# Linear attention and a gated feed-forward on one core: a k^T v product ahead of an attention run, weight sums beside chunk 0, and another order of a first layer's last steps

## The chip, the core and the metric

The kernel runs on one core of a Trainium2 chip. The engines of the core work side by side, each in its own order of instructions: TensorE (PE in the profile, its weight loads PEld), VectorE (DVE), ScalarE (ACT), GpSimd (POOL) and SyncE (SP, which here only issues DMAs). The metric is the time of the device in microseconds for one execution of the whole program; lower is better. Several runs are made and their median is told.

## The reference

```python
kv = np.einsum('bhsd,bhse->bhde', k, v)              # 8 batches, 8 heads, 576 tokens, 64 wide
out = np.einsum('bhsd,bhde->bhse', q, kv)
rms = np.sqrt(np.mean(out * out, axis=-1, keepdims=True) + 1e-06)
attn = (out / rms * g_norm)
x = np.ascontiguousarray(attn.transpose(0, 2, 1, 3)).reshape(4608, 512)
gate = 1.0 / (1.0 + np.exp(-(x @ w_gate)))           # 512 x 1536
val = x @ w_val                                      # 512 x 1536
return gate * val @ w_out                            # 1536 x 512
```

The weights come as 64-bit numbers and the rest as 32-bit ones; the kernel computes in 32 bits.

## The kernel before

**Chunks.** The 4608 tokens of the feed-forward are nine chunks of 512. The attention of batch b+1 is computed in pieces between the products of chunk b, since chunk b+1 needs its tokens. Chunk 0 uses plain products. Chunks 1 to 8 use a fast scheme with 26 products of block sums in place of 32 plain block products, for the first layer (gate and value, three column blocks j = 0, 1, 2) and for the second. Such a product needs *forms*: sums of blocks of the tokens (made by VectorE), of the hidden blocks h (`h_sums`, line 728: GpSimd, and for the last column block partly VectorE), of the first layer's weights (`w1_sums`, line 744, 28 sums of 128x256 for each column block, GpSimd, L747 in the profile) and of the second layer's weights (`w_form`, L1029 and L1031).

**The order is written by hand.** Every engine executes its instructions in the order in which the program text issues them. Around chunk 0 this order comes from the text `places` (line 802). Chunk 0's eleven tiles after the first have eight matmuls each; place p is the p-th of these 88 matmuls, 0.86 us apart, and behind it the named steps are issued: `CV` is one step of converting a weight unit (line 247), `KV2` the k^T v of batch 2, `D` the two ScalarE copies of it to `kvq` (L399, L400), `au ... ax1` and `bu ... bx1` the first and second attention run of batch 1 (products, squares, sums, root, norms, turns), `W0` the sums of first-layer weights of column block 0. In chunks 1 to 8 the steps are keyed to p, the number of the first layer's product (26 for each column block, 0 to 77), or to the place in the second layer.

**Converting weights.** A unit holds two 128x512 blocks. It takes five steps on VectorE (L197, L212, L224, L228, then L235 or L237) with two on ScalarE between them (L202 after the first, L217 after the second). Units 0 to 11 are the gate and value weights in the order of chunk 0's tiles: tile f needs unit f. Units 12 to 17 are the rows of the second layer's weights, two blocks each, in the order of chunk 0's second layer (L830 in the profile). `plain` (line 606) gives two PSUM banks to a tile; ScalarE's sigmoid (L599) and VectorE's product (L602) give them back.

**k^T v.** `kv_mm` (line 379, L388 and L395 in the profile) reads k and v from the tile h_more and writes a PSUM tile called `at`, which the attention runs use too, one after the other. The sums of first-layer weights write into parts of h_more, so they wait for the matmuls of batch 2's k^T v to read k and v. `kvq` holds the k^T v that the attention run's products (`u_mm`, L434) read.

**A first layer's end.** `PRODUCTS1` (line 671) lists 26 products: the PSUM region that a product adds to, the two forms, and the steps of `combine` (line 908) behind it. A step such as `o4=o4+K` adds region K to a piece of h (VectorE, L924), `s0` is a sigmoid (ScalarE, L913), and `o4*o0` multiplies value and gate (L916: GpSimd, but VectorE behind the very last product). Five PSUM banks go round: a region's bank is free once the last step that reads it is done. The second layer (L1058) starts at once; its first four regions take the bank of E, J, D and H of the first layer's end, in this order, and the product of its fourth region stands eighth and ninth among its first blocks of two matmuls each. The form 8 of h needs `o5`, form 9 needs `o7`, form 18 `o6` and `o4`.

**Chunk 1.** The weight sums of column block 2 are made late: 20 after the conversion's buffers are given up (line 885), and eight in chunk 1, one with each of p = 26 to 33 (lines 986, 987). There too the second layer's weight forms are made, on VectorE and GpSimd, each written over a piece of the first layer's weights that is used up and has been saved to DRAM, and each then stored to DRAM by SyncE.

Of the kernel before, what the change touches and what calls it, by code (L numbers as in the profile page):

```python
# [10 lines left out]
FP32 = mybir.dt.float32  # L11
# [9 lines left out]
def kernel(  # L21
# [11 lines left out]
    nc = tc.nc  # L33

    B, H, S, HD = q.shape
    T, DM = out.shape
    DF = moe_w_gate.shape[1]
    P = 128
# [17 lines left out]
    NRUN = NHP // 2  # L56
# [6 lines left out]
    NFT = DF // P  # L63
# [9 lines left out]
    const = ctx.enter_context(tc.tile_pool(name="const", bufs=1))  # L73
# [193 lines left out]


    kvq = const.tile([P, 2, NRUN, 2, HD], FP32, name="kvq")

    qTs = const.tile([P, QW], FP32, name="qTs")
    sqs = const.tile([P, 2 * NU * P], FP32, name="sqs")
# [102 lines left out]
    def feed(b):  # L375

        d = {}

        def kv_mm():
# [11 lines left out]
            for e in range(2):  # L391
                for m in range(NRUN):
                    for g in range(2):
                        rs, c = slice(PH * m, PH * m + PH), HD * (2 * g + e)
                        nc.tensor.matmul(ps[HD * g:HD * g + HD, m, e], rest[rs, c:c + HD],  # L395
                                         rest[rs, GH + c:GH + c + HD], start=False, stop=True, skip_group_check=True)

        def kv_copy():
            nc.scalar.copy(out=kvq[:, 0], in_=d["kv"])  # L399
            nc.scalar.copy(out=kvq[0:HD, 1], in_=d["kv"][HD:P])  # L400
# [82 lines left out]
            return ([u_mm, u_square, lambda: u_sum(0), lambda: u_sum(1), u_root] + norms +  # L483
                    [lambda i=i: x_turn(i) for i in range(NC)])

        kv = [kv_mm, kv_copy]
        t0, t1 = ([lambda m=m, e=e: turn(m, e) for e in range(2)] for m in range(NRUN))
        u0, u1 = heads_run(0), heads_run(1)
        if b == 1:
# [4 lines left out]
        where = """0:t00 5:t01 25:u0 26:q0 28:t10 30:s00,s01 33:t11 35:r0 36:n00 37:n01 39:n02 40:n03 42:n04 43:n05 44:n06  # L494
                   51:x00 52:x01 53:u1 56:q1 57:s10,s11 60:r1 62:n10,n11 63:n12 65:n13 66:n14 68:n15 69:n16""" if b == 2 else """
                   5:t00 8:t01 28:u0 29:t10 30:q0 33:s00,s01 36:r0 39:t11 41:n00 47:n01 51:x00,x01 54:u1
                   56:q1,s10,s11 61:r1 64:n10,n11""" if b == 3 else """
                   3:t00 7:t01 28:u0,t10 30:q0,s00,s01 37:r0 39:t11 47:n00,n01 53:x00,x01 54:u1
                   56:q1,s10,s11 60:r1 61:n10 63:n11"""
        first = [(int(w_.split(":")[0]), steps_[x]) for w_ in where.split() for x in w_.split(":")[1].split(",")]  # L500
# [133 lines left out]
    for token in order.split():  # L634
        name = token.rstrip("0123456789.")
        n = [int(i) for i in token[len(name):].split(".")]
        f = n[0]
# [10 lines left out]
        else:  # L648
            a[f][steps[name]]()
            if token == f"Q{NE - 1}":  # L650
# [10 lines left out]
    W_ORDER = (21, 24, 17, 18, 16, 25, 19, 42, 27, 34, 35, 36, 23, 29, 33, 20, 41, 28, 26, 40, 32, 38, 39, 43, 30, 37, 22,  # L661
               31)
# [17 lines left out]
    PRODUCTS2 = (("A", 8, 4, "o5=A"), ("C", 9, 1, "o4=C"), ("B", 18, 10, "o3=B"), ("A", 24, 14, "o1=A"),  # L680
# [7 lines left out]
    NPR = len(PRODUCTS2)  # L688
# [46 lines left out]
    NPA = len(PARTS)  # L735
    GW = 7 * 2 * P

    W1_FIRST = 20
    w1_more = [[] for _ in range(N3)]

    def w1_slot(j, s_):
# [2 lines left out]
    def w1_sums(j, some=slice(None)):  # L744
        for v in W_ORDER[some]:
            x, sign, y = SUMS[v]
            nc.gpsimd.tensor_tensor(out=w1_slot(j, w_at[v]), in0=w1_slot(j, w_at[x]), in1=w1_slot(j, w_at[y]),  # L747
                                    op=op_of(sign))
# [29 lines left out]
    def w1_form(c, j, part, v):  # L778
        if c == 1:
# [11 lines left out]
    spare_sg = sgs.pop()  # L791
    batch1, second_batch = feed(1), feed(2)
    named = {"LL": lambda: load_late(1), "LL2": lambda: load_late(2), "KV": batch1[0][0], "KV2": second_batch[0][0],
             "W0": lambda: w1_sums(0), "CV": convert_step}
    named.update({"C": batch1[0][1], "D": second_batch[0][1]})
    for i in range(NRUN):
        named[f"Q{i}"] = lambda i=i: load_q_run(1, i)
# [1 line left out]
    for i, which in enumerate("ab"):  # L799
# [3 lines left out]
        1:CV,CV 2:CV,Q0 4:CV,CV 5:CV,CV 6:CV,LL 7:CV,CV 10:CV,CV 11:Q1 15:CV 16:CV,CV 17:t00  # L803
        18:CV,CV 19:t01 20:KV 22:CV,CV,C 25:CV 26:CV,CV 29:au,LL2 30:CV
        31:asq 32:CV,t10,as0 34:CV,as1,art 35:CV 36:t11,arc,an0 37:an1 38:CV,an2 40:CV,CV 41:CV,ax0
        43:ax1 44:bu 46:CV,bsq 48:CV,CV,bs0 50:CV 52:CV,CV 54:bs1 55:CV,CV,brt 57:CV,CV 58:CV 60:CV,brc
        62:bn0,bn1 63:bn2 64:CV 65:CV,CV,CV 66:CV,CV 67:CV 68:KV2,D 71:bx0 72:CV 73:W0 75:bx1
        80:CV,CV,CV,CV,CV 84:CV 87:CV,CV
    """
    at_place = {}  # L810
    for some in places.split():
        p, names = some.split(":")
# [4 lines left out]
    for f in range(1, NFT):  # L817
        if f == NFT - 1:
            last = at_ps()
            ps = last[:, 0], last[:, 1]  # L820
        else:
            ps = mm_ps(), mm_ps()
        plain(0, f, ps, {at: at_place.get(2 * NMT * (f - 1) + at, ()) for at in range(2 * NMT)})
        if f == NFT - 1:
            w1_sums(1)

    ps = [mm_ps() for _ in range(G // P)]

# [37 lines left out]
    for f in range(0, NFT - 2, 2):  # L866
        for at in range(2 * G // P):
            second(at % (G // P), f + at // (G // P))
            if late:
                late.popleft()()  # L870
            if at % 4 < 3:
                convert_step()
            elif x_early:
                x_early.popleft()()
        if raw_ctx and not to_convert:
            raw_ctx.__exit__(None, None, None)
            raw_ctx = None
            sums = ctx.enter_context(tc.tile_pool(name="sums", bufs=1, side="right"))
            xs = sums.tile([P, 16, GH], FP32, name="xs")
            temps = sums.tile([P, 4, G], FP32, name="temps")  # L880
            ring_more = [sums.tile([P, N3 * DH], FP32, name=f"w_ring{i}") for i in range(2)]
            more_sgs = [sums.tile([P, G], FP32, name=f"sg{6 + i}") for i in range(2)]
            w1_more[2] = [t[:, 2 * P * i:2 * P * i + 2 * P] for t in ring_more + more_sgs
                          for i in range(t.shape[1] // (2 * P))]
            w1_sums(2, slice(W1_FIRST))
            x_early = deque(x_sums(1))
    assert raw_ctx is None
    kept3 = kept_pool.tile([15, P, N3 * DH], FP32, name="kept3")
# [45 lines left out]
    def first_layer_fast(c, at):  # L934
        for f in range(NFT):
            gv_tile(c, f)
        held = {}
        for j in range(N3):
            o = {f"t{n}": pair(temps[:, i]) for i, n in enumerate((0, 1, 8, 9))}
            for n in (3, 1, 2, 0):  # L940
                o[f"o{n}"] = pair(sg_tile())
            h = h_main[j].rearrange("p (g e t) c -> p g e (t c)", g=2, e=2)
            for n in range(4):
                o[f"o{4 + n}"] = h[:, :, n // 2, GH * (n % 2):GH * (n % 2) + GH]
            regions = {}
            for i, (name, hv, wv, steps) in enumerate(PRODUCTS1):
                part, p = next(n for n, r in enumerate(PARTS) if i in r), NPR * j + i
                new = name not in regions
                if new:
                    i_ = free.popleft()  # L950
                    regions[name] = i_, pair(bank(i_))
                ws = w1_form(c, j, part, hv)
                for g in range(2):
                    nc.tensor.matmul(regions[name][1][:, g], ws[:, g], xf[c][wv], start=(new and g == 0), stop=True,  # L954
                                     skip_group_check=True)
                combine(o, regions, steps, nc.vector if j == N3 - 1 and i == NPR - 1 else nc.gpsimd)
                give_all(regions, LAST1, i)
                for step in at.get(p, ()):
                    step()
                for _ in range(2 if i % HALF == HALF - 1 else 1):  # L960
                    if h_fill:
                        h_fill.popleft()[1]()
                if c > 1:
                    g_ = NPA * (N3 * (c - 2) + j) + part
                    if p < NPR * N3 - 1:
                        wait = (3 if part < 2 else 0) if j == 0 and c + 1 < B else 0
                        if wait and i == PARTS[part][-1]:
                            held[i + wait] = g_ + NPA
                        elif i == PARTS[part][-1]:
                            load_granule(g_ + NPA)  # L970
                        if j == 0 and i in held:
                            load_granule(held.pop(i))
                    if stores and p >= 24 and p % 2 == 0:
                        stores.popleft()()
                    k_, r = divmod(p - (38 if c == 2 else 20), 2)
                    if r == 0 and 0 <= k_ < NR:
                        load_w((c - 2) * NS + k_)
                else:
                    if p == 0:
                        keep_w1(0)  # L980
                        keep_w1(1)
                    elif p == NPR + HALF:
                        keep_w1(2)
                    if keeping:
                        keeping.popleft()()
                    if NPR <= p < NPR + len(W_ORDER) - W1_FIRST:
                        w1_sums(2, slice(W1_FIRST + p - NPR, W1_FIRST + p - NPR + 1))
            h_fill.extend(h_sums(j, slice(SUMS_FIRST) if j else slice(None)))

    tok = [slice(P * i, P * i + P) for i in range(NT)]  # L990
# [140 lines left out]
    for c in range(1, NG):  # L1131
# [15 lines left out]
                else:  # L1147
                    x_late.append((p - NPR, step))
        if c == 1:
            for at_, forms in ((at1, ((28, 9, 0), (30, 10, 0), (34, 12, 0), (52, 8, 1), (58, 14, 0), (64, 16, 1), (66, 11, 1), (74, 19, 0))), (at2, ((1, 13, 0), (2, 22, 0), (3, 23, 1), (4, 25, 1), (9, 15, 0), (10, 24, 0), (10, 20, 0), (11, 17, 0), (12, 18, 0), (13, 21, 0)))):  # L1150
                for p, n, pool_ in forms:
                    at_.setdefault(p, []).append(lambda n=n, eng=nc.gpsimd if pool_ else nc.vector, at_once=at_ is at1 or n == 13: w_form(n, eng, at_once))
        first_layer_fast(c, at1)
# [33 lines left out]
```

## Time and profile before

| What | us |
|---|---|
| median of 3 runs (lowest, highest) | 1011.74 (1011.13, 1013.35) |
| the profiled execution, its own time | 1010.92 |
| its span, first to last instruction | 1009.1 |
| TensorE busy | 995.6 |
| VectorE busy | 720.5 |
| GpSimd busy | 602.0 |
| ScalarE busy | 341.9 |
| chunk 0's products, last eleven tiles and attention | 28.2 to 116.2 |
| chunk 0's second layer | 116.2 to 157.4 |
| chunk 1 | 157.4 to 263.7 |
| granted TensorE clock | 1.0 |

A row of the timeline has the start in us from the span's beginning, the length, the engine, the line of the kernel, the operation, what is written and read, the shapes, and how many alike were merged; in brackets the engine's idle time before it and what ended it. A row of the groups has the count, the busy time, the mean length of one in ns, and the idle time before. A 32-bit product of 512 columns appears as two matmuls of 0.43 us, one of 256 columns as two of 0.216.

### The profile page before, as it was taken

The numbers are of one execution on the slowest core, as the hardware profiler recorded it, in microseconds if no ns is written. First come the engines' busy times: TensorE is split into PE (matmuls) and PEld (weight loads), VectorE is DVE, ScalarE is ACT, GpSimd is POOL, SyncE is SP. The second block draws the span as 40 slices with busy tenths as digits, with TensorE's granted clock in tenths as the row PEclk, the third lists the DMA queues.
The fourth block names the chain that finished last, engine by engine and source line by source line (L and its number), as shares of the span: only waits on it lengthen the run. The fifth ranks groups of instructions, "written<-read, shape, count | busy, mean of one in ns | idle before, by whom it ended". The sixth has DMA issues, their size and how long they took to land.

```text
span 1009.1 us, 16638 instructions
## 1 busy us (share of the span) xinstructions
PE 995.6 (99%) x5958; PEld 815.0 (81%) x5958; DVE 720.5 (71%) x1198; ACT 341.9 (34%) x605; POOL 602.0 (60%) x988
## 2 busy tenths in 40 slices
PE   8999999999999999999999999999999999999998
PEld 7454447888888888888888888888888888888887
DVE  4978998889768766784677566856587666755663
ACT  4567323651144213530344124421342133213320
POOL 1501999898358634955186707761595449644963
PEclk9999999999999999999999999999999999999999
DMA  9986415663889568746875577655864555445514
GB/s 264 291 242 214 149 42 155 203 222 109 274 288 278 167 179 241 235 153 198 264 228 170 174 226 248 190 170 182 254 205 133 166 181 201 153 150 170 211 46 121
DMA packets 156114, 195.43 MB, mean 194 GB/s; under 512 B 84832, under 2 KB 128864, under 8 KB 156032
## 3 DMA queue, kind: packets, MB, share of 16 engines
q0 software_dynamic: 22000, 114.11, 34.2%
q1 hardware_dynamic: 126864, 78.16, 27.7%
q10 hardware_dynamic: 7168, 2.10, 0.9%
q8 instruction: 47, 0.77, 0.3%
q14 instruction: 35, 0.29, 0.1%
HBM read 160.50 MB, written 25.56 MB: 184 GB/s over the span
## 4 chain that ended last, share of the span: by engine, by line
PE 70%; DVE 4%; DMA 1%; POOL 1%; issue 0%; DVEq 0%; POOLq 0%
PE mm L954 45%; PE mm L1058 22%; DVE h L924 2%; PE at L434 1%; DMA h_more<-in_v_dram 1%; DVE h L916 1%; PE at L388 1%; POOL h L728 1%; DVE temps L924 1%; POOL h_more L728 0%; PE at L395 0%; DMA xT<-xTs 0%; POOL w_ring L1029 0%; DVE w L1029 0%; DVE w L1031 0%
## 5 line engine op out<-in xcount | busy, mean ns | idle before, releaser
L954 PE MATMUL mm<-xs,w 128*128 128x256 f32 x1428 | 332.0, 380 | 0.5 <-DVE temps L924 0.5
L954 PEld LDWEIGHTS mm<-xs,w 128*128 128x128 f32 x1428 | 270.4, 190 | 37.9 <-DVE temps L924 0.9
L954 PE MATMUL mm<-xT,w 128*128 128x256 f32 x948 | 229.9, 380 | 0.0
L954 PEld LDWEIGHTS mm<-xT,w 128*128 128x128 f32 x948 | 179.5, 190 | 25.2 <-issue 0.5
L924 DVE TENSOR_TENSOR sg<-sg,mm 128x512 f32<-128x512 f32 (+1 forms) x176 | 100.8, 600 | 93.5 <-PE mm L954 43.2
L776 POOL DMA_DIRECT2D w<-kept x84 | 46.8, 557 | 194.5 <-PE mm L954 192.0
L1058 PE MATMUL mm<-w,h 128*128 128x256 f32 x630 | 143.4, 379 | 0.5 <-POOL h L916 0.4
L1058 PEld LDWEIGHTS mm<-w,h 128*128 128x128 f32 x630 | 119.5, 190 | 17.5 <-POOL h L916 0.8
L920 ACT COPY temps<-mm 128x512 f32<-128x512 f32 (+1 forms) x128 | 66.1, 538 | 186.9 <-PE mm L1058 94.7
L916 POOL TENSOR_TENSOR h<-h,sg 128x512 f32<-128x512 f32 x72 | 91.0, 1283 | 50.0 <-DVE h L924 30.4
L728 POOL TENSOR_TENSOR h<-h 128x128 f32<-128x128 f32 x216 | 112.2, 531 | 12.7 <-DVE h_more L728 9.2
L1058 PE MATMUL mm<-w,h_more 128*128 128x256 f32 x474 | 109.9, 381 | 2.9 <-DVE h L924 2.9
L913 ACT ACTIVATE sg<-sg 128x512 f32<-128x512 f32 x96 | 59.7, 630 | 133.2 <-DVE sg L924 133.2
L1058 PEld LDWEIGHTS mm<-w,h_more 128*128 128x128 f32 x474 | 89.5, 190 | 17.6 <-DVE h L924 5.7
L920 ACT COPY sg<-mm 128x512 f32<-128x512 f32 (+1 forms) x112 | 57.0, 510 | 91.9 <-PE mm L1058 53.6
L728 POOL TENSOR_TENSOR h_more<-h 128x128 f32<-128x128 f32 x120 | 63.7, 534 | 40.4 <-DVE h L916 36.1
L924 DVE TENSOR_TENSOR temps<-temps,mm 128x512 f32<-128x512 f32 (+1 forms) x96 | 59.4, 619 | 26.8 <-PE mm L1058 17.4
L594 PE MATMUL mm<-xT,w 128*128 128x512 f32 x176 | 77.8, 596 | 0.1
L920 ACT COPY h<-mm 128x512 f32<-128x512 f32 x48 | 28.1, 586 | 139.8 <-PE mm L954 126.0
L924 DVE TENSOR_TENSOR temps<-mm,temps 128x512 f32<-128x512 f32 (+1 forms) x64 | 39.8, 622 | 49.7 <-PE mm L1058 23.3
L924 DVE TENSOR_TENSOR sg<-mm,sg 128x512 f32<-128x512 f32 (+1 forms) x64 | 39.6, 619 | 45.1 <-PE mm L954 23.6
L594 PEld LDWEIGHTS mm<-xT,w 128*128 128x128 f32 x176 | 32.6, 190 | 39.2 <-issue 36.4
(142 smaller groups left out, 1267.5 us busy)
## 6 DMA issues: line engine op xcount, KB each, us to landing
w<-kept POOLq DMA_DIRECT2D x42, 896.0 KB, 5.2
w<-kept POOLq DMA_DIRECT2D x90, 384.0 KB, 4.4
w<-kept POOLq DMA_DIRECT2D x42, 768.0 KB, 5.2
out_dram<-sg SPq DMA_DIRECT2D x119, 64.0 KB, 1.7
h_more<-in_k_dram SPq DMA_DIRECT2D x28, 256.0 KB, 5.4
h_more<-in_v_dram SPq DMA_DIRECT2D x28, 256.0 KB, 6.1
q<-in_q_dram SPq DMA_DIRECT2D x96, 72.0 KB, 4.8
xT<-xTs SPq DMA_DIRECT2D x96, 72.0 KB, 4.1
```

Of the source, the lines that this page charges most:

```text
L388: nc.tensor.matmul(ps[HD * g:HD * g + HD, m, e], mains[2 * m + g, "k"][:, c], mains[2 * m + g, "v"][:, c], start=(e == 0 and j == 0), stop ...
L434: nc.tensor.matmul(u[HD * e:HD * e + HD, o:o + HD], qTs[HD * g:HD * g + HD, c:c + HD], kvq[HD * g:HD * g + HD, t == NSL, m, e], start=True ...
L594: nc.tensor.matmul(self.ps[i], w[("wg", "wv")[i], self.f][:, m, :], xT[self.c][:, m, :], start=(m == 0), stop=(m == NMT - 1), skip_group_c ...
L728: ops.append((eng, lambda v=v, x=x, sign=sign, y=y, eng=eng: eng.tensor_tensor(out=h_form(v, j), in0=h_form(x, j), in1=h_form(y, j), op=op ...
L776: nc.gpsimd.dma_start(out=granule(g)[:, 0:n], in_=kept1[g // NPA % N3, g % NPA][:, 0:n])
L913: nc.scalar.activation(out=o["o" + step[1]], in_=o["o" + step[1]], func=AF.Sigmoid)
L916: mult.tensor_tensor(out=o[x], in0=o[x], in1=o[y], op=ALU.mult)
L920: nc.scalar.copy(out=o[out_], in_=o[expr])
L924: tt(out=o[out_], in0=o[x], in1=o[y], op=ALU.add if sign == "+" else ALU.subtract)
L954: nc.tensor.matmul(regions[name][1][:, g], ws[:, g], xf[c][wv], start=(new and g == 0), stop=True, skip_group_check=True)
L1058: nc.tensor.matmul(regions[name][1], h_form(hv, j), ws[:, j], start=(used[i] and j == 0), stop=(j == N3 - 1), skip_group_check=True)
```

## The change

- The k^T v of batch 2 goes from place 68 to place 44, ahead of the second attention run of batch 1, whose products go from place 44 to 47 and squares from 46 to 48. As `kvq` is still needed by that run, a new step `ASIDE` copies the product out of PSUM to a tile of its own, `kv_ahead`; `D` then copies from there to `kvq`, at place 55 in place of 68.
- `W0`, the sums for column block 0, goes from place 73 to 46; `W1`, for block 1, from behind chunk 0's last tile to place 74. The sums of block 2 are all made in one piece where 20 of them stood; the eight in chunk 1 are gone.
- The steps behind the last product of a first layer have another order.
- In chunk 2 the second part of a norm (`n11`) goes from place 64 to 66.
- In chunk 1 five weight forms of the second layer have other places: 11 from 66 to 52, 14 from 58 to 57, 8 from 52 to 58, 19 from 74 to 61 (16 stays at 64). Those with a 1 at the end are GpSimd's.

```diff
+    kv_ahead = const.tile([P, NRUN, 2, HD], FP32, name="kv_ahead")
...
+        def kv_set_aside():
+            nc.scalar.copy(out=kv_ahead, in_=d["kv"])
+            d["kv"] = kv_ahead
+
         def kv_copy():
             nc.scalar.copy(out=kvq[:, 0], in_=d["kv"])
...
-        kv = [kv_mm, kv_copy]
+        kv = [kv_mm, kv_copy, kv_set_aside] if b == 2 else [kv_mm, kv_copy]
...
-                   56:q1,s10,s11 61:r1 64:n10,n11""" if b == 3 else """
+                   56:q1,s10,s11 61:r1 64:n10 66:n11""" if b == 3 else """
...
-                 ("K", 43, 2, "o7=o7-t8 o7*o3 o4=o4+K o4*o0 o6=H+t8 o6*o2"))
+                 ("K", 43, 2, "o4=o4+K o7=o7-t8 o4*o0 o6=H+t8 o6*o2 o7*o3"))
...
-    W1_FIRST = 20
...
-             "W0": lambda: w1_sums(0), "CV": convert_step}
+             "W0": lambda: w1_sums(0), "W1": lambda: w1_sums(1),
+             "ASIDE": second_batch[0][2], "CV": convert_step}
...
-        43:ax1 44:bu 46:CV,bsq 48:CV,CV,bs0 50:CV 52:CV,CV 54:bs1 55:CV,CV,brt 57:CV,CV 58:CV 60:CV,brc
-        62:bn0,bn1 63:bn2 64:CV 65:CV,CV,CV 66:CV,CV 67:CV 68:KV2,D 71:bx0 72:CV 73:W0 75:bx1
+        43:ax1 44:KV2,ASIDE 46:CV,W0 47:bu 48:CV,CV,bsq 50:CV,bs0 52:CV,CV 54:bs1 55:CV,CV,brt,D 57:CV,CV 58:CV 60:CV,brc
+        62:bn0,bn1 63:bn2 64:CV 65:CV,CV,CV 66:CV,CV 67:CV 71:bx0 72:CV 74:W1 75:bx1
...
-        if f == NFT - 1:
-            w1_sums(1)
...
-            w1_sums(2, slice(W1_FIRST))
+            w1_sums(2)
...
-                    if NPR <= p < NPR + len(W_ORDER) - W1_FIRST:
-                        w1_sums(2, slice(W1_FIRST + p - NPR, W1_FIRST + p - NPR + 1))
...
-(52, 8, 1), (58, 14, 0), (64, 16, 1), (66, 11, 1), (74, 19, 0)
+(52, 11, 1), (57, 14, 0), (58, 8, 1), (61, 19, 0), (64, 16, 1)
```

More of the change, by code (lines that the diff above doesn't have):

```diff
@@ L1149 @@
         if c == 1:
-            for at_, forms in ((at1, ((28, 9, 0), (30, 10, 0), (34, 12, 0), (52, 8, 1), (58, 14, 0), (64, 16, 1), (66, 11, 1), (74, 19, 0))), (at2, ((1, 13, 0), (2, 22, 0), (3, 23, 1), (4, 25, 1), (9, 15, 0), (10, 24, 0), (10, 20, 0), (11, 17, 0), (12, 18, 0), (13, 21, 0)))):
+            for at_, forms in ((at1, ((28, 9, 0), (30, 10, 0), (34, 12, 0), (52, 11, 1), (57, 14, 0), (58, 8, 1), (61, 19, 0), (64, 16, 1))), (at2, ((1, 13, 0), (2, 22, 0), (3, 23, 1), (4, 25, 1), (9, 15, 0), (10, 24, 0), (10, 20, 0), (11, 17, 0), (12, 18, 0), (13, 21, 0)))):
                 for p, n, pool_ in forms:
```

## The prediction, made before the result was known

> **What bounds the kernel now.** I read the page first: TensorE is busy for 995.6 of 1009.1 us at full granted clock, so only holes in its row can be won, and a new hole costs at once. The view of who waited for whom, for TensorE alone, names the holes:
>
> ```profile
> engine line waited for: us in total, times, longest us
> PE mm L1058 <- DVE h L924: 3.2, 8, 0.8
> ...
> PE at L388 <- ACT sqs L474: 1.0, 1, 1.0
> PE mm L954 <- DVE temps L924: 0.5, 1, 0.5
> PE mm L1058 <- POOL h L916: 0.4, 1, 0.4
> ```
>
> All four are touched. The most frequent is seen in the timeline of chunk 2, where the first layer (L954) hands over to the second (L1058); columns are start, length, engine:
>
> ```profile
> 336.49 1.03 PE L954 MATMUL mm<-xT,w 128*128 128x256 f32 x4
> ...
> 337.36 2.32 PE L1058 MATMUL mm<-w,h 128*128 128x256 f32 x10
> 337.42 0.69 DVE L924 TENSOR_TENSOR h<-h,temps 128x512 f32<-128x512 f32 x1
> 338.21 0.69 DVE L916 TENSOR_TENSOR h<-h,sg 128x512 f32<-128x512 f32 x1
> 338.82 0.68 DVE L924 TENSOR_TENSOR h<-h,mm 128x512 f32<-128x512 f32 x1
> ...
> 339.53 0.69 DVE L916 TENSOR_TENSOR h<-h,sg 128x512 f32<-128x512 f32 x1
> 340.14 0.68 DVE L924 TENSOR_TENSOR h<-mm,temps 128x512 f32<-128x512 f32 x1
> ...
> 340.88 2.42 PE L1058 MATMUL mm<-w,h_more 128*128 128x256 f32 x10 [0.34 <-DVE h L924]
> ```
>
> The DVE rows are the last product's steps in their written order; 340.14 is `o6=H+t8`. Region E of the second layer takes the bank that H gives back, so the matmul waits until 340.14+0.68.
>
> The cost side is VectorE in chunk 0, which converts the weights. Its groups of instructions, first in 76.4 to 98.0 us with GpSimd idle, then in 98 to 129 us with GpSimd forming weight sums:
>
> ```profile
> L228 DVE SCALAR_TENSOR_TENSOR cz<-st,cz 128x1024 uint32<-128x1024 uint32 x3 | 3.6, 1217 | 0.1
> L197 DVE TENSOR_SCALAR w<-st 128x1024 uint32<-128x1024 uint32 x4 | 2.7, 680 | 0.0
> ```
>
> ```profile
> L228 DVE SCALAR_TENSOR_TENSOR cz<-st,cz 128x1024 uint32<-128x1024 uint32 x4 | 7.0, 1742 | 0.0
> L197 DVE TENSOR_SCALAR w<-st 128x1024 uint32<-128x1024 uint32 x4 | 4.3, 1085 | 0.0
> L602 DVE TENSOR_TENSOR h<-mm,sg 128x512 f32<-128x512 f32 x3 | 2.0, 682 | 0.9 <-ACT sg L599 0.9
> ```
>
> The reader sees the same conversion steps 0.4 to 0.5 us longer each beside GpSimd, and the step that reads PSUM (L602) unchanged. How late they may be, the timeline shows (last step of units 11 and 12, then first use):
>
> ```profile
> 103.33 1.68 DVE L235 SCALAR_TENSOR_TENSOR w<-w,g_col,cz 128x1024 f32<-128x1024 f32 x1
> 112.02 1.63 DVE L237 TENSOR_TENSOR w<-w,cz 128x1024 f32<-128x1024 f32 x1
> ```
>
> ```profile
> 109.28 7.03 PE L594 MATMUL at<-xT,w 128*128 128x512 f32 x16
> 116.15 41.36 PE L830 MATMUL mm<-w,h 128*128 128x512 f32 x96
> ```
>
> **The change, part by part.** All times are of the profiled execution: 1010.92 us, 1009.1 in its span; it stands 0.8 below the median 1011.74, to which I add the sum.
>
> *Last steps' order.* With S the second layer's start (337.36), `o4=o4+K` can begin 0.2 after K's matmuls end, as `t8+D` does after D's, so at S+0.2. Steps on VectorE begin 0.61 apart, or 0.7 to 0.8 where one needs the one before (the rows above). `o6=H+t8` is then fourth and ends near S+2.8; region E is wanted 14 matmuls of 0.216 after S, at S+3.0, and the hole closes. Each hole is 0.51 late (340.88 against 339.51+4x0.216) plus a first matmul that takes 0.32 instead of 0.216: 0.61. There are seven, one in each of chunks 2 to 8: -4.3. What is late next: `o7*o3` goes from second to last and ends near S+4.7, instead of S+1.5; the last block of the product with form 9 needs it at S+5.2 (343.14 in the trace, less 0.6). The DVE sums behind it start when they did, 341.88. In the other two column blocks the same order goes to GpSimd, and nothing there is read before the second layer: 0.
>
> *Chunk 1's hand-over.* It has the same hole (1.0 late at 232.51) and one for GpSimd's `o5*o1` (0.56 late at 229.24), with 0.1 after each: 1.8. GpSimd's form 11 at place 66 ran from 224.16, right ahead of it, and eight weight sums (0.7 to 1.5 each in 185 to 196 us, about 8) stood in its queue. Both go ahead; DVE's form 19 (1.23 at 226.41) leaves the tail for place 61. Both causes gone: -1.8; if one stays, about half. Form 19 now waits for GpSimd's form 11 (place 52): GpSimd ends that near 212, place 61 is near 214. SP issues one store for each form, as before, only in another order, and the saves of those w1 slots went out by 206.5: 0.
>
> *n11 two places later, chunk 2.* DVE's two norms (0.71 each from 327.41) stand before the step that frees a bank; one moves behind: the stop at 329.48 (0.63 late, and 0.1) goes: -0.7. The bound is 0 if the next bank is then late.
>
> *k^T v of batch 3 at place 44.* Its 80 matmuls (2.5 us) only move. Its wait of 1.0 at 97.26, for the norms that held the PSUM tile, goes; at place 44 the tile is free at 73.1, matmuls come at 74.1, and its loads landed by 66.5. One copy more on ACT (0.35, row L399) and the two to kvq now ahead of a gate: 0.7 on ACT, whose next consumer on TensorE is over 6 us away. -1.1 with the restart. No DMA is moved.
>
> *The sums beside chunk 0.* They wait for that k^T v (56.2 us of GpSimd idle at L747), so they start near 75 instead of 98.03; GpSimd's queue holds nothing else there. The 56 sums of blocks 0 and 1 (98 to 158) end near 144. Of a conversion unit's five steps, a unit beside them takes 7.3 us (106.28 to 113.57), without them 4.9 of work (42.82 to 48.35 less 0.6 of waiting). In 76.4 to 98 stand three units and one step: 3x2.4+0.5 = 7.7 more; VectorE's 3.0 us of idle there are used up: some 4.8 later from 98 on, where it has no idle left until 145.8. TensorE's wants, 1.0 earlier than now, are 108.3, then a tile (6.87) later each:
> - unit 11: 105.0+4.8 = 109.8, 1.5 late;
> - unit 12: 113.65+4.8 = 118.4 against 116.7, 1.8 late;
> - unit 13: 121.1+4.8 = 125.9 against 125.3, 0.6 (to 1.5) late;
> - unit 14: 133.1 against 132.8, 0.3; unit 15: in time.
>
> That is 4.2 to 5.2, with restarts and a late gate 5.0: +5.0. The third block's 28 sums then run from about 151, in place of 20 from 159 and eight later; they share with the x sums what the second block's shared before: 0, bounds ±1.
>
> Here a rule can be weighed. The row says +0.5 for a step. The Trainium skill, "SBUF — State Buffer", section "Who interferes with whom", says that VectorE with two SBUF inputs or a two-port mode and GpSimd exclude each other for a whole instruction; L602, with one SBUF input, agrees with 682 ns.
>
> Sum: -4.3-1.8-0.7-1.1+5.0 = -2.9: 1008.0 for such an execution, **1008.9** as median. The clock is 1.0 throughout and stays.
>
> **The rivals.**
> - *The cover holds.* VectorE's lateness is only half (2.4), because steps wait for ACT anyhow. Then unit 11 is in time, unit 12 0.9 and unit 13 0.6 late: +1.5 in place of 5.0, the lower bound of this cost: 1005.3. For it: 0.6 waits for ACT in each undisturbed unit. Against: VectorE ran without idle beside GpSimd.
> - *The hole moves* (slower). `o7*o3`, now last, ends 1.1 later than I reckon, past S+5.8, and TensorE loses the same 0.6 a little later in all eight chunks. It decides from S+5.2 on. Then -4.3 and 1.2 of the 1.8 are not had: 1014.3. For it: the step took 0.91 beside GpSimd where it stood last (340.93). Against: 0.5 in hand.
> - *Whole blocking.* Each of the 16 conversion steps in 76.4 to 98 waits for one whole sum, 0.73 (GpSimd's L747 alone), not 0.5: 16x0.23 = 3.7 more lateness, paid in full, the upper bound of this cost: 1012.5. For it: L228's 0.53. Against: L197's 0.41. By the Trainium skill's rule just named this is what the loser of each issue would pay, and the sum would be +0.8 in place of -2.9.
> - *It does not do what it says in chunk 1:* GpSimd stays behind and both holes there remain: 1010.6. For it: it ran some 6 us behind its places there. Against: 8 us leave its queue.
>
> **How the numbers follow.** Forecast 0.50 (1007.4 to 1010.4 by itself), cover 0.17, hole moves 0.10, whole blocking 0.10, chunk 1 0.13. The range leaves out the hole that moves and about half of the cover and of the blocking case: 1005.2 to 1012.4. About 0.2% (2.0 us) is what a measurement of this kernel can tell from no change; it lies at 1009.7 and 1013.8. Faster: 0.37 of the forecast, 0.17 and 0.02 of the chunk-1 case, 0.56. Slower: 0.08 of the moved hole, 0.03 of blocking, 0.11. Within: 0.33.
>
> **What would show it.** In the profile after: no TensorE wait for DVE h at L1058, none for ACT at L388; GpSimd's sums from about 75; L228 near 1.74 us already in 76 to 98; new TensorE waits for DVE w at L594 and L830 of about 5 us together; the second layers of chunks 2 to 8 0.6 shorter. Wrong it would be if those new waits are under 3 or over 7, or if a new wait for DVE's L916 or L728 stands at L1058.

## The result, and the profile after

The changed kernel takes 1005.38 us in the median of 8 runs (1004.44 to 1009.63), against 1011.87 for the kernel before in 8 runs beside it: a ratio of 0.9946, with a 95% interval of 0.993 to 0.9963. That is 6.5 us by the medians and 5.5 by the ratio. The forecast was 2.9 faster, 1008.9, with a range from 1005.2 to 1012.4: the sign is right, the range holds the time at its very edge (1005.38 against 1005.2), and about half of the gain was missing from the sum (2.6 of 5.5 us by the ratio, 3.6 of 6.5 by the medians). The profiled execution takes 1004.44 us, its span 1002.7, at a granted clock of 1.0.

First what the forecast said would go. TensorE's waits after:

```profile
engine line waited for: us in total, times, longest us
...
PE mm L833 <- DVE w L237: 0.7, 3, 0.4
...
PE mm L1059 <- POOL h L733: 0.3, 1, 0.3
PE at L389 <- DMA h_more<-in_v_dram: 0.2, 1, 0.2
```

(The lines moved: L1058 is L1059 now, L954 is L957, L924 is L927, L916 is L919, L830 is L833, L602 is L607, L728 is L733, L388 is L389.) The eight waits of the second layer for VectorE, the one for GpSimd's product and the one of batch 2's k^T v are gone. Three waits are new, in chunk 0's second layer, for a converted weight unit: 0.72 us together, where the prediction had about 5 and called itself wrong under 3. New too is the wait for a GpSimd form (L733), 0.33 at 253.27; it lies in the middle of chunk 1's second layer and not at the hand-over. The hand-over of chunk 2 in the timeline after:

```profile
335.48 1.03 PE L957 MATMUL mm<-xT,w 128*128 128x256 f32 x4
...
336.35 2.32 PE L1059 MATMUL mm<-w,h 128*128 128x256 f32 x10
336.55 0.69 DVE L927 TENSOR_TENSOR h<-h,mm 128x512 f32<-128x512 f32 x1 [0.17 <-PE mm L957]
337.15 0.69 DVE L927 TENSOR_TENSOR h<-h,temps 128x512 f32<-128x512 f32 x1
337.75 0.68 DVE L919 TENSOR_TENSOR h<-h,sg 128x512 f32<-128x512 f32 x1
...
338.36 0.68 DVE L927 TENSOR_TENSOR h<-mm,temps 128x512 f32<-128x512 f32 x1
338.50 3.19 PE L1059 MATMUL mm<-w,h_more 128*128 128x256 f32 x14
...
339.14 1.51 DVE L919 TENSOR_TENSOR h<-h,sg 128x512 f32<-128x512 f32 x2
```

With S at 336.35, `o4=o4+K` starts at S+0.20, `o6=H+t8` ends at S+2.7 (forecast 2.8), and the matmuls for forms in h_more run through as 14 where they were 4 and 10. `o7*o3`, now last, ends at S+4.3.

Now the cost side: VectorE's groups in 76.4 to 98 us, where GpSimd now forms sums, and TensorE at chunk 0's end.

```profile
L228 DVE SCALAR_TENSOR_TENSOR cz<-st,cz 128x1024 uint32<-128x1024 uint32 x3 | 4.7, 1564 | 0.0
L197 DVE TENSOR_SCALAR w<-st 128x1024 uint32<-128x1024 uint32 x3 | 2.9, 977 | 0.0
L607 DVE TENSOR_TENSOR h<-mm,sg 128x512 f32<-128x512 f32 x2 | 1.4, 685 | 0.4 <-ACT sg L604 0.4
```

```profile
108.68 7.03 PE L599 MATMUL at<-xT,w 128*128 128x512 f32 x16
116.06 7.10 PE L833 MATMUL mm<-w,h 128*128 128x512 f32 x16 [0.35 <-DVE w L237]
123.38 7.13 PE L833 MATMUL mm<-w,h 128*128 128x512 f32 x16 [0.21 <-DVE w L237]
130.67 27.73 PE L833 MATMUL mm<-w,h 128*128 128x512 f32 x64 [0.16 <-DVE w L237]
158.24 1.03 PE L957 MATMUL mm<-xT,w 128*128 128x256 f32 x4
```

The steps did become longer, but L228 has a mean of 1564 ns, not 1742, and tile 11 (108.68) is not held up at all.

The stages of both profiled executions and of all variants, from the starts of TensorE's rows. "Start-up" is the start of the seventeenth matmul of 512 columns, "chunk 0" goes from there to chunk 1's first product, "second layers" is that of chunks 2 to 7 each (the last chunk's is 0.2 shorter to its last matmul), "k, v" the sum of TensorE's waits for the k and v of later batches:

| Kernel | start-up | chunk 0 | chunk 1, first + second layer | chunk 2, first | second layers | k, v |
|---|---|---|---|---|---|---|
| before | 31.17 | 126.18 | 70.46 + 35.85 | 73.70 | 34.28 | 0.93 |
| after | 31.71 | 126.53 | 70.36 + 34.27 | 73.48 | 33.67 | 0.22 |
| order alone (a1) | 33.19 | 126.66 | 71.24 + 34.96 | 75.06 | 33.67 | 2.15 |
| H third (a2) | 31.43 | 125.44 | 70.48 + 35.71 | 74.77 | 34.13 | 0.74 |
| chunk 0 part alone (a3) | 31.41 | 127.26 | 70.81 + 36.13 | 74.69 | 34.28 | 0.66 |
| narrow sums (a4) | 33.59 | 125.03 | 70.36 + 34.28 | 72.96 | 33.67 | 0 |
| all but the chunk 0 part (b1) | 31.25 | 125.82 | 71.22 + 34.44 | 74.40 | 33.67 | 1.00 |
| sums in halves (b2) | 32.95 | 125.04 | 70.36 + 34.27 | 74.55 | 33.67 | 1.74 |
| old form places (b3) | 31.47 | 126.44 | 71.01 + 35.53 | 73.44 | 33.67 | 0.18 |
| third block split (b4) | 33.50 | 127.19 | 71.21 + 34.44 | 73.88 | 33.67 | 0.62 |
| changed, again (c1) | 31.33 | 127.21 | 70.36 + 34.30 | 74.29 | 33.67 | 1.04 |
| halves, again (c2) | 31.75 | 125.03 | 70.36 + 34.29 | 72.96 | 33.67 | 0 |
| halves, no chunk 0 part (c3) | 34.44 | 125.25 | 74.51 + 34.44 | 73.83 | 33.67 | 1.40 |
| quarters (c4) | 33.20 | 125.03 | 88.36 + 34.28 | 72.96 | 33.67 | 0.48 |

Each row is one execution; a2, a4, b3 and b4 were run only once, so that for these four only the stages are read and not the time.

Before against after, the span's 6.4 us are: +0.5 start-up, +0.35 chunk 0, -1.7 chunk 1, -0.2 chunk 2's first layer, seven times -0.6 in the second layers, and -1.25 in chunk 4's first layer (74.21 to 72.96), where the wait for k and v of 0.93 did not come this time. (The tail behind the last matmul is 0.1 longer.)

### The profile page after: what moved, and what is told of

The parts are those of the page before. It is cut to its first block, busy times and chain, and to the rows that moved or that the text cites. A ratio compares the mean times of both kernels' runs of the same rounds, so it can differ in the third digit from the quotient of the medians.

```text
span 1002.7 us, 16624 instructions
## 1 busy us (share of the span) xinstructions
PE 993.8 (99%) x5958; PEld 815.8 (81%) x5958; DVE 722.1 (72%) x1198; ACT 342.5 (34%) x606; POOL 617.5 (62%) x988
## 3 DMA queue, kind: packets, MB, share of 16 engines
q0 software_dynamic: 22000, 114.11, 34.4%
## 4 chain that ended last, share of the span: by engine, by line
PE 73%; POOL 2%; DMA 1%; issue 0%; SPq 0%; DVE 0%; POOLq 0%
PE mm L957 46%; PE mm L1059 24%; PE at L439 1%; POOL h L733 1%; PE at L389 1%; DMA h_more<-in_v_dram 1%; POOL w_ring L1030 0%; POOL h_more L733 0%; PE at L396 0%; SPq L134 0%; POOL w L780 0%; DVE sg L927 0%; POOLq L780 0%; POOLq L1030 0%
## 5 line engine op out<-in xcount | busy, mean ns | idle before, releaser
L957 PE MATMUL mm<-xs,w 128*128 128x256 f32 x1428 | 331.8, 380 | 0.0
L957 PEld LDWEIGHTS mm<-xs,w 128*128 128x128 f32 x1428 | 270.5, 190 | 37.1
L957 PE MATMUL mm<-xT,w 128*128 128x256 f32 x948 | 229.8, 380 | 0.0
L957 PEld LDWEIGHTS mm<-xT,w 128*128 128x128 f32 x948 | 179.5, 190 | 25.0 <-issue 0.5
L927 DVE TENSOR_TENSOR sg<-sg,mm 128x512 f32<-128x512 f32 (+1 forms) x176 | 100.7, 599 | 85.5 <-PE mm L957 41.5
L1059 PE MATMUL mm<-w,h 128*128 128x256 f32 x630 | 143.1, 379 | 0.3 <-POOL h L733 0.3
L1059 PEld LDWEIGHTS mm<-w,h 128*128 128x128 f32 x630 | 119.6, 190 | 17.0 <-POOL h L733 0.7
L919 POOL TENSOR_TENSOR h<-h,sg 128x512 f32<-128x512 f32 x72 | 96.0, 1350 | 57.0 <-DVE h L927 31.0
L733 POOL TENSOR_TENSOR h<-h 128x128 f32<-128x128 f32 x216 | 112.1, 531 | 16.6 <-DVE h_more L733 13.1
L1059 PE MATMUL mm<-w,h_more 128*128 128x256 f32 x474 | 108.2, 379 | 0.0
L916 ACT ACTIVATE sg<-sg 128x512 f32<-128x512 f32 x96 | 59.7, 630 | 131.5 <-DVE sg L927 131.5
L1059 PEld LDWEIGHTS mm<-w,h_more 128*128 128x128 f32 x474 | 90.1, 190 | 12.2
L733 POOL TENSOR_TENSOR h_more<-h 128x128 f32<-128x128 f32 x120 | 61.6, 517 | 34.3 <-DVE h L919 30.0
L927 DVE TENSOR_TENSOR temps<-temps,mm 128x512 f32<-128x512 f32 (+1 forms) x96 | 59.4, 619 | 25.9 <-PE mm L1059 16.6
L927 DVE TENSOR_TENSOR temps<-mm,temps 128x512 f32<-128x512 f32 (+1 forms) x64 | 39.8, 622 | 50.9 <-PE mm L1059 23.6
L927 DVE TENSOR_TENSOR sg<-mm,sg 128x512 f32<-128x512 f32 (+1 forms) x64 | 39.7, 620 | 45.1 <-PE mm L957 24.5
```

What stands on the lines that cost most here:

```text
L733: ops.append((eng, lambda v=v, x=x, sign=sign, y=y, eng=eng: eng.tensor_tensor(out=h_form(v, j), in0=h_form(x, j), in1=h_form(y, j), op=op ...
L916: nc.scalar.activation(out=o["o" + step[1]], in_=o["o" + step[1]], func=AF.Sigmoid)
L919: mult.tensor_tensor(out=o[x], in0=o[x], in1=o[y], op=ALU.mult)
L927: tt(out=o[out_], in0=o[x], in1=o[y], op=ALU.add if sign == "+" else ALU.subtract)
L1059: nc.tensor.matmul(regions[name][1], h_form(hv, j), ws[:, j], start=(used[i] and j == 0), stop=(j == N3 - 1), skip_group_check=True)
```

## Experiments

### Which step the second layer waits for

*The order alone (a1)*, in the kernel before:

```diff
-                 ("K", 43, 2, "o7=o7-t8 o7*o3 o4=o4+K o4*o0 o6=H+t8 o6*o2"))
+                 ("K", 43, 2, "o4=o4+K o7=o7-t8 o4*o0 o6=H+t8 o6*o2 o7*o3"))
```

> Kernel before with the new order of the last steps alone. Theory (the second layer's fourth region waits for the bank of H, which o6=H+t8 gives back): the stop at the hand-over of chunks 2 to 8 goes, 0.61 each, and the one of 1.1 in chunk 1; GpSimd's 0.66 in chunk 1 stays. 4.3 to 5.4 us faster than before, and no TensorE wait for DVE h at L1058 is left. Rival (the hole only moves to the step that is now last, o7*o3): no gain, a new wait of 0.3 to 0.8 behind the first fifteen matmuls of each second layer.

Measured: ratio 0.9964 (0.9951 to 0.9977), some 3.6 us, less than the 4.3 to 5.4 expected. The second layers of chunks 2 to 7 are 33.67 each, as in the whole change, and TensorE waits for no VectorE h there. The hole did not move. Chunk 1, though, gains only 0.1 (106.20 against 106.31): its second layer is 0.9 shorter, its first layer 0.8 longer, with a new stop of 0.43 at 214.41. It stands where the third column block begins:

```profile
210.00 3.74 POOL L916 TENSOR_TENSOR h<-h,sg 128x512 f32<-128x512 f32 x3
213.77 0.59 ACT L920 COPY sg<-mm 128x512 f32<-128x512 f32 x1 [1.11 <-POOL h L916]
214.41 1.13 PE L954 MATMUL mm<-xs,w_ring 128*128 128x256 f32 x4 [0.43 <-ACT sg L920]
```

The three L916 are GpSimd's last products of the second column block, and `o7*o3` is now the last of them. In chunk 1 five `sg` tiles, the buffers for `o0` to `o3`, go round, and a column block takes four, so the next block's second one, for `o1=A`, is the tile that `o7*o3` still reads. With the eight weight sums in its queue GpSimd gets there late. All of the 0.8 arises there, between 213.8 and 215.8. The prediction had "nothing there is read before the second layer: 0" for the new order in these column blocks; the value is not read, but its buffer is wanted.

*One step moved (a2)*:

```diff
-                 ("K", 43, 2, "o7=o7-t8 o7*o3 o4=o4+K o4*o0 o6=H+t8 o6*o2"))
+                 ("K", 43, 2, "o7=o7-t8 o7*o3 o6=H+t8 o4=o4+K o4*o0 o6*o2"))
```

> Kernel before with one step moved: o6=H+t8 from fifth to third place (behind o7*o3); o7 is multiplied as early as before, o4 and K's bank come later than before. If the bank of H alone is what is awaited: the stops go as in a1, second layers of chunks 2 to 8 each 33.67 us instead of 34.28. If it is K's bank or o4 and its sums 21 and 24: they stay at 34.3 or grow.

What TensorE waits for at the hand-overs now:

```profile
PE mm L1058 <- POOL h_more L728: 2.0, 8, 0.7
```

The wait for VectorE's `o6=H+t8` is gone, as the bank alone would have it; but `o4`, one step later, makes GpSimd late with the forms built on it (21 and 24 at L728), and eight waits for those stand in its place: 34.13 for a second layer, 0.15 of the 0.6 won. So the explanation by the bank holds, and it needs a second half that the prediction did not have: `o4` was next in line, and the changed order works because it puts `o4=o4+K` first *and* `o6=H+t8` fourth.

### What the chunk 0 part is worth

*Alone (a3)*, from the changed kernel:

```diff
-                 ("K", 43, 2, "o4=o4+K o7=o7-t8 o4*o0 o6=H+t8 o6*o2 o7*o3"))
+                 ("K", 43, 2, "o7=o7-t8 o7*o3 o4=o4+K o4*o0 o6=H+t8 o6*o2"))
...
-                   56:q1,s10,s11 61:r1 64:n10 66:n11""" if b == 3 else """
+                   56:q1,s10,s11 61:r1 64:n10,n11""" if b == 3 else """
...
-(52, 11, 1), (57, 14, 0), (58, 8, 1), (61, 19, 0), (64, 16, 1)
+(52, 8, 1), (58, 14, 0), (64, 16, 1), (66, 11, 1), (74, 19, 0)
```

> Only the chunk 0 part: k^T v of batch 3 at place 44, sums of column blocks 0 and 1 beside chunk 0, the third block's in one piece; last steps, n11 and chunk 1's weight forms as in the kernel before. Theory now: the wait of 1.1 goes, three new stops cost 1.4, and GpSimd's hole in chunk 1 (0.66) goes: between 1.0 faster and 0.5 slower than before. The recorded prediction's step, 5.0 us of new stops in chunk 0: 3 to 4 us slower. Rival that the sums beside chunk 0 cost nothing: 1.1 to 1.8 faster.

Measured: 1.002 (1.0009 to 1.0031), 2.0 us slower than before. This is outside all three expectations: more than 0.5 slower, less than the 3 to 4 of the prediction's step, and no gain. In the profile, chunk 0 is 1.1 longer (three stops of 0.98, 0.21 and 0.13) and chunk 1 is 0.6 longer: one wait of 1.8 for VectorE's h at 234.47 stands where waits of 0.40 and 0.84 were. Why VectorE is later there than before stays open.

*Everything else without it (b1)*, the changed kernel with `KV2,D` at place 68, `W0` at 73, the second block's sums behind the last tile and the third's split:

```diff
-        43:ax1 44:KV2,ASIDE 46:CV,W0 47:bu 48:CV,CV,bsq 50:CV,bs0 52:CV,CV 54:bs1 55:CV,CV,brt,D 57:CV,CV 58:CV 60:CV,brc
-        62:bn0,bn1 63:bn2 64:CV 65:CV,CV,CV 66:CV,CV 67:CV 71:bx0 72:CV 74:W1 75:bx1
+        43:ax1 44:bu 46:CV,bsq 48:CV,CV,bs0 50:CV 52:CV,CV 54:bs1 55:CV,CV,brt 57:CV,CV 58:CV 60:CV,brc
+        62:bn0,bn1 63:bn2 64:CV 65:CV,CV,CV 66:CV,CV 67:CV 68:KV2,D 71:bx0 72:CV 73:W0 75:bx1
```

> Kernel before with everything but the chunk 0 part: new order of the last steps, n11 later, chunk 1's weight forms at their new places. k^T v of batch 3, the sums of blocks 0 and 1 and the split third block stay as before. Theory: chunks 2 to 8 gain as in the whole change (4.3 and 0.6), chunk 1 gains nothing or loses up to 1, because GpSimd still has the eight sums in its queue when VectorE's form 19 asks for its form 11: 3.9 to 5 us faster than before. Rival (the chunk 0 part adds nothing to the others): chunk 1 takes 104.6 us as in the whole change, and the gain is 6 to 7 us.

Measured: 0.9955 (0.9938 to 0.9971), which can't be told from the whole change (0.9946, and 0.9956 in c1). By stages it is 0.7 faster in chunk 0 (125.82 against 126.53; the wait at k^T v was 0.64 in this execution) and 1.0 slower in chunk 1 (105.66 against 104.63). Chunk 0 varies from execution to execution: 125.44 to 126.66 with the old places (before, a1, a2, b1), as the wait at k^T v is 0.27 to 1.22 there, and 126.44 to 127.26 with the sums beside it (after, a3, b3, b4, c1). By the means of these the chunk 0 part costs 0.9 in chunk 0, about what it gives to chunk 1.

The theory had the place in chunk 1 wrong. No stop is left at b1's hand-over; the loss is in the first layer (71.22), the stop of a1 again, 0.42 at 211.60.

### What made chunk 1 faster

*Old places of the forms (b3)* and *the third block's sums split again (b4)*, each in the changed kernel:

```diff
-(52, 11, 1), (57, 14, 0), (58, 8, 1), (61, 19, 0), (64, 16, 1)
+(52, 8, 1), (58, 14, 0), (64, 16, 1), (66, 11, 1), (74, 19, 0)
```

```diff
-            w1_sums(2)
+            w1_sums(2, slice(20))
...
+                    if NPR <= p < NPR + len(W_ORDER) - 20:
+                        w1_sums(2, slice(20 + p - NPR, 21 + p - NPR))
```

> The changed kernel with chunk 1's second-layer weight forms at the places of before. Theory (GpSimd's form 11 and VectorE's form 19 in the tail hold up the hand-over): chunk 1's second layer 0.6 to 2 us longer than 34.27, with a TensorE wait for GpSimd or VectorE at L1059 near 230 us. Rival (the eight sums alone were in the way): chunk 1 stays at 104.6 us.

> The changed kernel, but the third block's sums split as before: 20 in one piece, eight one by one in chunk 1. Theory (their 8 us in GpSimd's queue push form 11 and so form 19 late): chunk 1 takes 0.5 to 2 us more than 104.6. Rival (moving the forms alone was enough): 104.6.

Chunk 1 takes 106.54 us in b3 and 105.65 in b4, against 104.63. In b3 a hole at the hand-over is back (232.85), for VectorE alone, and a stop of 0.41 for VectorE stands ahead of it, at 227.11:

```profile
PE mm L1059 <- DVE h L927: 0.8, 1, 0.8
```

In b4 the hand-over has no stop. Of the 1.0, 0.85 is in the first layer (71.21 against 70.36), with the stop of a1 at 215.22 (0.41): the theory's number came, but not by form 11 and form 19, so that it fits is luck. In chunk 1 b4 is as long as b1 (105.66): what the chunk 0 part gives to chunk 1 is room to make the eight sums earlier. Whether they could be made earlier without the chunk 0 part was not run.

So the places of the forms are worth 1.9 and the eight sums 1.0 in the presence of the other; with old places and the old order, taking the eight sums away (a3) gained nothing. The forecast's 1.8 came out (1.7) only for order, forms and eight sums together; the order alone gave 0.1 (a1), and forms without the order were not run.

### What the sums beside the conversion cost, and how

*Narrow sums (a4)*:

```diff
+            n = 2 * P if j == 2 or w_at[v] >= 24 else 16
-            nc.gpsimd.tensor_tensor(out=w1_slot(j, w_at[v]), in0=w1_slot(j, w_at[x]), in1=w1_slot(j, w_at[y]),
-                                    op=op_of(sign))
+            nc.gpsimd.tensor_tensor(out=w1_slot(j, w_at[v])[:, 0:n], in0=w1_slot(j, w_at[x])[:, 0:n],
+                                    in1=w1_slot(j, w_at[y])[:, 0:n], op=op_of(sign))
```

> The changed kernel, but the weight sums of column blocks 0 and 1 take 16 of their 256 columns (so most of the first layer's forms are left out and the output is not the reference's). Theory: VectorE's conversion steps are slow only because GpSimd's sums run beside them; with short sums they fall back to about 0.68 and 1.22 us, the three TensorE waits for DVE w (0.35, 0.21, 0.16 us) go, and the first product of chunk 1 starts some 1.4 us earlier than 158.24. Rival (the three waits come from the chain VectorE, ScalarE, VectorE of a conversion unit by itself): the waits stay.

Of the 56 sums 48 are narrow here (the slots from 24 on stay whole). TensorE has no wait at L833 left, chunk 0 takes 125.03, and chunk 1's first product starts at 158.63 only because this execution's start-up was 1.9 later. So the stops come from the sums, and they cost 1.5 us in the profile after (126.53), 2.2 in c1 (127.21), and 1.4 to 2.2 over all five executions that have them.

*Sums in halves (b2, c2)* and *in quarters (c4)*, the changed kernel with each sum of the first two blocks in shorter pieces (quarters: four of 64 columns):

```diff
-            nc.gpsimd.tensor_tensor(out=w1_slot(j, w_at[v]), in0=w1_slot(j, w_at[x]), in1=w1_slot(j, w_at[y]),
-                                    op=op_of(sign))
+            for n in ((slice(0, P), slice(P, 2 * P)) if j < 2 else (slice(None),)):
+                nc.gpsimd.tensor_tensor(out=w1_slot(j, w_at[v])[:, n], in0=w1_slot(j, w_at[x])[:, n],
+                                        in1=w1_slot(j, w_at[y])[:, n], op=op_of(sign))
```

> The changed kernel with each sum of column blocks 0 and 1 made in two halves of 128 columns. Theory (a conversion step that comes right behind another one waits for one whole GpSimd instruction): such steps take some 0.25 us more than undisturbed in place of 0.5, L228 about 1.5 instead of 1.74, the waits for DVE w at L833 go or shrink below 0.2 in all, and it is 0.5 to 1.5 us faster than the changed kernel. Rival (the two engines share the path by the byte): L228 stays near 1.74 and the time stays.

> The changed kernel beside its variants on one chip. 5 to 7 us faster than the kernel before; chunk 0 from the end of the start-up to chunk 1 some 126.5 us with three TensorE waits for DVE w at L833. The waits for batches' k and v at L389, none to two of 0.2 to 1.5 us in other profiles, come and go.

> The changed kernel with the sums of column blocks 0 and 1 in halves of 128 columns. Theory (a step waits for one whole GpSimd instruction): 1 to 2 us faster than the changed kernel, chunk 0 at 125.0 us without a wait at L833. Rival (the gain of the earlier look was chance): the same as the changed kernel.

> The changed kernel with the sums of column blocks 0 and 1 in quarters of 64 columns. Theory: a step right behind another takes some 0.15 us more than undisturbed (L228 1.35 to 1.4), GpSimd needs longer for all (224 short instructions), chunk 0 stays at 125.0 us as there is no stop left to win: within 0.1% of the halves. Rival (sharing by the byte): L228 back near 1.74.

VectorE's step L228 in 76.4 to 129 us, four kernels in turn, by the width of GpSimd's sums: 256 columns (the changed kernel), 128 (c2), 64 (c4), 16 (a4). The last numbers are busy us and the mean ns of one step:

```profile
L228 DVE SCALAR_TENSOR_TENSOR cz<-st,cz 128x1024 uint32<-128x1024 uint32 x7 | 11.7, 1667 | 0.0
```

```profile
L228 DVE SCALAR_TENSOR_TENSOR cz<-st,cz 128x1024 uint32<-128x1024 uint32 x7 | 10.2, 1452 | 0.0
```

```profile
L228 DVE SCALAR_TENSOR_TENSOR cz<-st,cz 128x1024 uint32<-128x1024 uint32 x7 | 9.4, 1338 | 0.0
```

```profile
L228 DVE SCALAR_TENSOR_TENSOR cz<-st,cz 128x1024 uint32<-128x1024 uint32 x7 | 8.6, 1228 | 0.1
```

The bytes that GpSimd moves are the same in the first three. The step's extra time follows the length of *one* GpSimd instruction: 0.52, 0.25 and 0.12 us for those steps that are slowed (1.74, 1.47, 1.34 against 1.22), where one sum by itself takes 0.73, 0.45 and 0.31. It is 0.2 less than one instruction each time. Sharing by the byte is out. So is, by an estimate, sharing by GpSimd's pace, which is lower with short sums (0.90 and 1.24 in place of 0.73 for a whole sum): the extra time would then be about 0.42 and 0.31, not 0.25 and 0.12. The Trainium skill, "SBUF — State Buffer", section "Who interferes with whom", says that where these two engines contend, one shuts the other out for a whole instruction, and the runs agree but for the 0.2.

With halves the stops go (chunk 0 125.03, no wait at L833), and it is the fastest kernel here. b2 has a ratio of 0.9937 (0.9918 to 0.9957) to the kernel before, with a median of 1002.72. Side by side on one chip c2 has a ratio of 0.9927 (0.9914 to 0.994) and c1, the changed kernel, one of 0.9956 (0.9942 to 0.9969); the medians are 1003.02 and 1005.91. In quarters the stops are gone too, but GpSimd runs out of time. The same number of bytes takes it until 175.9 for two blocks, in place of 146.4, and its gate products of chunk 1's first column block begin at 197.95 in place of 177.28. The row of TensorE in its timeline, with the wait ahead of it in brackets:

```profile
203.54 2.07 PE L958 MATMUL mm<-xs,h_more 128*128 128x256 f32 x4 [15.15 <-ACT sg L924]
```

and that of GpSimd's first gate products in chunk 1:

```profile
197.95 4.92 POOL L920 TENSOR_TENSOR h<-h,sg 128x512 f32<-128x512 f32 x4
```

One stop of 15.15 us, and a ratio of 1.0106 (1.009 to 1.0122): the expectation "within 0.1% of the halves" missed it, since it weighed VectorE's steps alone.

*Halves without the chunk 0 part (c3)*: b1 with the same edit as b2.

> Kernel before with the new order of last steps, n11 and chunk 1's weight forms, the sums of blocks 0 and 1 in halves, and without the chunk 0 part. GpSimd gets more instructions and starts them late (98 us), with the eight sums of block 3 still in chunk 1. Theory (the chunk 0 part is worth what it takes off GpSimd's queue in chunk 1, about 1.0, and the wait of 1.1 at k^T v, once its own stops are gone): 1 to 2.5 us slower than the changed kernel in halves. Rival (the chunk 0 part is worth nothing): the same.

Measured: 1.0 (0.9988 to 1.0013), all of the gain lost, 7.7 us behind c2 by the medians and far outside the 1 to 2.5 expected. Of the 9.2 between the two profiled executions 4.3 are chunk 1 (108.95 against 104.65, with a stop of 2.8 at 192.63): GpSimd starts on the sums at 100 and comes to its gate products of chunk 1 at 186.31, in place of 178.19 in c2, and the stop is again a `sg` tile that it still reads. The rest lies in the start-up (34.44 against 31.75) and in waits for k and v (1.40 against none) of these two executions, which vary in all kernels; how much of it belongs to c3 stays open. What the chunk 0 part buys, then, is time for GpSimd, and that is worth little with long sums and much with short ones.

## Why the prediction came out as it did

| Term of the sum | forecast | measured |
|---|---|---|
| last steps' order, chunks 2 to 8 | -4.3 | -4.3 (34.28 to 33.67 in six, 0.62 in the last; a1) |
| chunk 1's hand-over | -1.8 | -1.7, for order, forms and eight sums together (b3, b4) |
| n11 two places later | -0.7 | -0.7 (73.70 to 72.96 where no k or v was awaited) |
| k^T v at place 44 | -1.1 | -1.15 (126.18 to 125.03 without stops); 0.4 to 1.6 by a1, a2 and b1 |
| the sums beside chunk 0 | +5.0 | +1.5; 1.4 to 2.2 in five executions (a4, c1) |
| wait for later k and v | none | 0 to 2.15 in any kernel |

The measured terms add up to -6.4 with 1.5 for the sums, -5.7 with 2.2, and the result (-5.5 by the ratio, -6.5 by the medians) lies near both. The range held it by luck: it reached down to half of the rival "the cover holds", and that rival's reason is not what happened.

The step that failed is "three units and one step: 3x2.4+0.5 = 7.7 more" and with it "some 4.8 later from 98 on". VectorE was 3.6 us late when unit 11's first step began (99.73 against 96.11), 2.8 at the end of unit 11 (107.85 against 105.01) and 2.3 at that of unit 12 (115.92 against 113.65): unit 11 was in time for tile 11, units 12 to 14 late by 0.35, 0.2 and 0.2. The rival "the cover holds" has nearly these numbers (2.4 late, +1.5). But waits for ACT did not do it; the count of slowed steps did: the three units took 1.2, 1.9 and 1.9 us more than undisturbed, in place of 2.4 each. The timeline after, VectorE and then GpSimd:

```profile
80.21 0.68 DVE L607 TENSOR_TENSOR h<-mm,sg 128x512 f32<-128x512 f32 x1
80.81 1.21 DVE L228 SCALAR_TENSOR_TENSOR cz<-st,cz 128x1024 uint32<-128x1024 uint32 x1
...
85.45 0.74 DVE L447 TENSOR_REDUCE ms<-sqs 128x9 f32<-128x576 f32 x1
86.11 0.68 DVE L212 TENSOR_SCALAR cz<-st 128x1024 uint32<-128x1024 uint32 x1
86.75 1.74 DVE L224 SCALAR_TENSOR_TENSOR w<-st,w 128x1024 f32<-128x1024 uint32 x1
```

```profile
80.84 1.77 POOL L751 TENSOR_TENSOR h_more<-w,h_more 128x256 f32<-128x256 f32 x1
```

A conversion step right behind another one pays one GpSimd instruction, less 0.2 (86.75: 1.74). A step right behind an instruction that is itself not slowed beside GpSimd (L607 from PSUM, a reduction) mostly does not: L228 at 80.81 takes its 1.21, L212 at 86.11 its 0.68, and at 80.84 it is GpSimd's sum that takes 1.77 in place of 0.73. Behind a turn (L462, L464) it is mixed: 0.64 at 109.13, but 1.68 at 106.17, 0.4 more than undisturbed. Of the 16 steps from 76.56 to 99.73, six stand behind something other than a conversion step, and five of these six are slowed by 0.25 us at most. All 16 together took 5.5 more than undisturbed, not 7.7. The unit at 106.28 to 113.57, from which I took 7.3, has only a turn ahead of it and then its five steps in a row; but two rows behind it showed the rule before the result was known: 114.17 (L197, 0.68) and 119.88 (L237, 1.21), steps of unit 13 behind L602, undisturbed beside GpSimd. The price was right for that stage and was carried to a stage with another neighbourhood. The Trainium skill, "SBUF — State Buffer", section "Who interferes with whom", also has "Issue order, not op shape, decides who blocks", and the trace agrees at 80.81 and 80.84. The rows by themselves say the same; I had reckoned how long a wait is and not which of the two waits.

"The hole moves" was wrong: `o7*o3` ends 0.9 before it is wanted (S+4.3 against S+5.2). "Whole blocking" was wrong in its price (0.52 for a slowed step, not 0.73) and in its count. "It does not do what it says in chunk 1" was wrong for the whole change, and is what happens when parts are left out (a1, a3, b3). The 0 for the new order in the other column blocks failed as well (a1, b1, b4: 0.8 in chunk 1's first layer); in the whole change it costs nothing only because the eight sums are gone.

## What to carry to other kernels

When two engines shut each other out by whole instructions, the price of running them side by side was here one instruction of the other, less 0.2 us, for each step that follows directly on another such step; it must be counted in the order of the stage where it will be paid, and it can be made smaller by cutting the other engine's instructions, as long as that engine has the time (halves won 2.9 us, quarters lost 15). Steps behind a layer's last product should be ordered by what the next layer asks for first, and that is a PSUM bank or a buffer as well as a value: moving only the bank's step put the next waiter in its place (a2), and the product moved to the end held a buffer too long when its engine was late (a1). A change of several parts may have none that carries the gain of a stage alone; b1 and a3 show that the part with the most moved work was not the one that gained.

## What the runs showed that was not expected

- An extra time that is a GpSimd instruction's length less 0.2 us, for 256, 128 and 64 columns (0.52, 0.25, 0.12).
- A buffer that the last step of a column block lets go of cost 0.8 us in chunk 1 when GpSimd was late (a1, b1, b4). The long stops of c3 (2.8) and c4 (15.15) wait for such a buffer too.
- TensorE's waits for the k and v of later batches appear in other chunks from kernel to kernel, 0 to 2.15 us in all, and the start-up ends between 31.2 and 34.4 us (with 1.7 of waiting for q in a4, and 2.6 behind VectorE's L346 in c3). Together they are as large as some of the effects measured. A difference of 2 us between two single profiles must be read by stages.
